# A gate and value stage on five blocks of 768 or 1024 tokens, with its two groups side by side and two of their sums made in PSUM

## The chip, the cores and the metric

One core of a Trainium2 chip runs the whole program. Matrix products run on TensorE (PE in the profile, its weight loads PEld), element-wise work on VectorE (DVE) and ScalarE (ACT), and SyncE (SP) issues the DMA transfers. Operands lie in SBUF, matmuls write to PSUM, which has eight banks of 512 fp32 columns, and large intermediates go through memory. The metric is the device time of one execution in microseconds.

## The reference, cut to what matters

```
x    = attention(q, k, v, g_norm)        # linear attention and RMS norm; 4608 tokens of 512
h    = x @ w_in                          # 512 -> 2048
x    = (h * clip(h + 3, 0, 6) / 6) @ w_out       # 2048 -> 512        (MLP1)
g    = x @ w_gate;  val = x @ w_val      # 512 -> 1536 each          (the stage that is changed)
out  = (silu(g) * val) @ w_out2          # 1536 -> 512                (the output stage)
```

The inputs are float64; the kernel decodes the weights itself.

## The kernel before

Precision comes from splits: a float32 operand is kept as a high and a low part (`h...`, `l...`; L109 on ScalarE makes the high part, L110 on VectorE the low one), and a product is three matmuls, low x high, high x low and high x high. Products of 256 x 256 blocks use a 2 x 2 scheme with seven products for eight: of the x operand seven combinations are needed (B11, B21, B22 and the sums T1 to T4), of the weights seven as well. `product` (L604-613) issues one of the seven: two 128-row pieces of the contraction times three matmuls, six in all.

The program goes through attention, MLP1 in nine blocks of 512 tokens, the gate and value stage, and the output stage in nine blocks of 512. In MLP1's last block the first weights of the next stage are decoded and split (`load_second`), and its last outputs `x1o` are copied from the accumulators `acc_8_0` to `acc_8_3`, the even ones by ScalarE, the odd ones by VectorE (L514-516).

The gate and value stage has six blocks of 768 tokens, in halves of 384 (TH). They are visited forwards with one half of the weights and backwards with the other. At each visit three steps are done, `gv_step`, each for 256 gate and 256 value features: a group `quad` (L721-744) for gate, then one for value. A group is 7 products x 6 matmuls = 42 matmuls of 384 columns in four PSUM banks, so that two groups have all eight. Its sums are made in SBUF: ScalarE copies a product out (L731, L734, L743), VectorE adds the others (L732, L736, L739 to L741). Then come Silu (L748, 1536 columns), the product of both halves (L750, 1536 columns) and the store to `g2d` (L751).

For the next block `load_x1` loads x in one transfer of 1536 KB at the first of a visit's three steps, and `prepare_x` makes sums and splits behind the third. Seven operand pairs lie in the pools `x1` (six tiles, right side of SBUF) and `x2` (eight tiles, left side). Beside the steps, further weights are built (forward half), stored to `wsd` and loaded again at the turn, and the output weights W2 are built (backward half). At the end `g_first` and `g_one` load the output stage's first blocks of `g2d`.

TensorE runs its instructions in the order in which the code issues them; ScalarE's, VectorE's and SyncE's order is set by a scheduler when the program is built. Every engine takes its own in order, so that one that waits holds up all behind it.

## Time and profile before

| | |
|---|---|
| Runs | 1676.84, 1676.83, 1675.19 us; median 1676.83 |
| Profiled execution | 1677.94 us, of which the span of the trace is 1676.1 |
| TensorE busy | 1656.5 us, 99% of the span, 10640 matmuls |
| VectorE, ScalarE busy | 1300.5 us (78%), 851.5 us (51%) |
| Gate and value stage | 864.12 to 1397.60 us after the span's start, 3024 matmuls |

All rows are of the profiled execution. A timeline gives start and duration of each instruction; matmuls overlap in it, since the next starts before the one before has left the array, so that what a matmul costs is the distance between two starts. A name stands without its number (`q_g` for the gate group's banks, `hT` for the high part of a T operand).

### The profile page before, as it was taken

Reading aid. Unit: us, or ns where it says so; the run is one execution under the profiler, and the core shown is the slowest. Engines: PE = TensorE matmul, PEld = TensorE weight load, DVE = VectorE, ACT = ScalarE, POOL = GpSimd, SP = SyncE. Lnnn points to the kernel's source line nnn. Section 1 sums busy time; section 2 is a strip of 40 time slices with the busy share of each in tenths; the row PEclk is TensorE's granted clock in tenths of the full one; section 3 lists DMA queues with packets and bytes.
Section 4 is the critical chain, followed back from the end, with each engine's and each line's share of the span. In section 5 each row is a group of like instructions: output and inputs, shape, how many; then the busy total and the mean of one; then the engine's idle time right before and its main releaser. Section 6 shows DMA issues by size and latency. Waiting matters only on the chain.

```text
span 1676.1 us, 27991 instructions
## 1 busy us (share of the span) xinstructions
PE 1656.5 (99%) x10640; PEld 1526.4 (91%) x10640; DVE 1300.5 (78%) x2472; ACT 851.5 (51%) x1553; POOL 2.4 (0%) x7
## 2 busy tenths in 40 slices
PE   8999999999999999999999999999999999999999
PEld 4567889889989989998889999999999999999999
DVE  6887997677787777777889988678897776877874
ACT  5876554444454444545666555445555444444432
POOL 0000000000000000000000000000000000000000
PEclk9999999999999999999999999999999999999999
DMA  8885444444445454335464544475553357655642
GB/s 231 273 262 163 142 147 136 147 141 147 139 122 160 130 151 119 126 101 201 150 202 163 204 154 157 165 270 194 182 189 131 133 207 275 214 190 195 219 152 101
DMA packets 224998, 288.63 MB, mean 172 GB/s; under 512 B 80992, under 2 KB 139360, under 8 KB 224864
## 3 DMA queue, kind: packets, MB, share of 16 engines
q1 hardware_dynamic: 220480, 285.80, 52.5%
q8 instruction: 83, 1.36, 0.3%
q10 hardware_dynamic: 4384, 1.05, 0.3%
q14 instruction: 51, 0.42, 0.1%
HBM read 211.03 MB, written 75.76 MB: 171 GB/s over the span
## 4 chain that ended last, share of the span: by engine, by line
PE 82%; DVE 9%; DMA 3%; ACT 3%; issue 2%; SPq 0%; DVEq 0%; ACTq 0%
PE q_g L608 14%; PE q_v L608 14%; PE acc L113 7%; PE a L608 7%; PE acc L114 7%; PE acc L115 7%; PE c L608 4%; PE d L608 4%; PE o2c L856 3%; PE o2d L856 3%; PE o2a L856 3%; PE h L119 2%; PE o2e L856 2%; DMA graw<-g2d 1%; PE kv L291 1%
## 5 line engine op out<-in xcount | busy, mean ns | idle before, releaser
L113 PE MATMUL acc<-g,wo 128*128 128x512 f32 x512 | 202.1, 395 | 0.0
L114 PE MATMUL acc<-g,wo 128*128 128x512 f32 x512 | 199.7, 390 | 0.0
L115 PE MATMUL acc<-g,wo 128*128 128x512 f32 x512 | 199.5, 390 | 0.0
L653 ACT ACTIVATE t<-h,three 128x512 f32<-128x512 f32 x120 | 86.9, 724 | 141.4 <-DVE h L650 107.7
L109 ACT ACTIVATE g<-t 128x512 fp32r<-128x512 f32 x142 | 89.5, 630 | 65.3 <-DVE t L654 55.8
L110 DVE TENSOR_TENSOR g<-t,g 128x512 fp32r<-128x512 f32 x142 | 96.7, 681 | 31.6 <-ACT g L109 30.8
L115 PEld LDWEIGHTS acc<-g,wo 128*128 128x128 f32 x512 | 96.1, 188 | 20.4
L113 PEld LDWEIGHTS acc<-g,wo 128*128 128x128 f32 x512 | 96.2, 188 | 20.2 <-DVE g L110 0.4
L114 PEld LDWEIGHTS acc<-g,wo 128*128 128x128 f32 x512 | 96.2, 188 | 18.3
L654 DVE SCALAR_TENSOR_TENSOR t<-t,h 128x512 f32<-128x512 f32 x120 | 82.4, 687 | 30.7 <-ACT t L653 29.3
L608 PE MATMUL q_v<-hT,v 128*128 128x384 f32 x288 | 73.6, 336 | 0.0
L743 ACT ACTIVATE hg<-q_g 128x384 f32<-128x384 f32 x36 | 17.7, 492 | 105.3 <-PE q_g L608 105.3
L750 DVE TENSOR_TENSOR hv<-hg,hv 128x1536 f32<-128x1536 f32 x36 | 63.1, 1753 | 5.5 <-ACT hv L743 5.5
L732 DVE TENSOR_TENSOR h1v<-h1v,q_v 128x384 f32<-128x384 f32 x36 | 19.9, 554 | 54.6 <-ACT h1v L731 53.4
L119 PE MATMUL h<-x,w_i 128*128 128x512 f32 x128 | 57.8, 594 | 1.4 <-DVE w_i L202 0.7
L743 ACT ACTIVATE hv<-q_v 128x384 f32<-128x384 f32 x36 | 17.7, 492 | 79.5 <-PE q_v L608 79.5
L608 PE MATMUL q_v<-hB,v 128*128 128x384 f32 x216 | 55.1, 336 | 0.0
L608 PE MATMUL a<-T,wh_i 128*128 128x256 f32 x240 | 53.4, 285 | 1.6 <-ACT s L627 1.4
L109 ACT ACTIVATE gxh<-gt 128x1024 fp32r<-128x1024 f32 x26 | 27.4, 1054 | 54.0 <-DVE gt L784 54.0
L748 ACT ACTIVATE hg<-hg 128x1536 f32<-128x1536 f32 x36 | 53.5, 1487 | 0.9
L109 ACT ACTIVATE gyh<-gb 128x512 fp32r<-128x512 f32 x54 | 32.3, 623 | 41.2 <-DMA gb<-g2d 40.8
L608 PE MATMUL c<-T,wh_i 128*128 128x256 f32 x240 | 53.0, 283 | 0.0
(618 smaller groups left out, 5460.3 us busy)
## 6 DMA issues: line engine op xcount, KB each, us to landing
wo<-wod SPq DMA_DIRECT2D x128, 512.0 KB, 3.4
g2d<-hv SPq DMA_DIRECT2D x36, 768.0 KB, 3.7
graw<-g2d SPq DMA_DIRECT2D x26, 1024.0 KB, 7.3
xr<-x1d SPq DMA_DIRECT2D x10, 1536.0 KB, 7.1
gb<-g2d SPq DMA_DIRECT2D x54, 256.0 KB, 4.9
x1d<-x1o SPq DMA_DIRECT2D x36, 256.0 KB, 2.8
out_dram<-o SPq DMA_DIRECT2D x36, 256.0 KB, 2.5
raw_i<-in_moe_w_in_dram SPq DMA_DIRECT2D x16, 512.0 KB, 5.5
```

What stands on the lines that cost most here:

```text
L109: nc.scalar.activation(out=hi, in_=src, func=AF.Copy)
L110: nc.vector.tensor_tensor(out=lo, in0=src, in1=f32(hi), op=ALU.subtract)
L113: nc.tensor.matmul(out_, wh, xl, start=start, stop=False)
L114: nc.tensor.matmul(out_, wl, xh, start=False, stop=False)
L115: nc.tensor.matmul(out_, wh, xh, start=False, stop=stop)
L119: nc.tensor.matmul(out_, f32(w), f32(x), start=start, stop=stop)
L608: nc.tensor.matmul(ps, a[:, kk], b[kk] if isinstance(b, list) else b[:, kk], start=first and n == 0, stop=n == 5, skip_group_check=True,)
L653: nc.scalar.activation(out=t, in_=h[i], func=AF.Relu, bias=three[:, 0:1])
L654: nc.vector.scalar_tensor_tensor(out=t, in0=t, scalar=6.0, in1=h[i], op0=ALU.min, op1=ALU.mult)
L748: nc.scalar.activation(out=hg, in_=hg, func=AF.Silu)
L750: nc.vector.tensor_tensor(out=hv, in0=hg, in1=hv, op=ALU.mult)
L856: nc.tensor.matmul(ps[:, i * TO2:(i + 1) * TO2], a[:, cs], b, start=first and i == 0 and n == 0, stop=n == 2, skip_group_check=True,)
```

## The change

The stage now has five blocks, with halves of 384, 512, 512, 384 and 512 tokens (SPANS), ten visits and 30 steps. In a step gate and value are computed together: each of the seven products is issued for gate, then for value, in the order A11 B11, S1 T1, S2 T2, S4 B22, S3 T3, A12 B21, A22 T4, and all eight banks belong to one step. Two sums of a group come about in PSUM: ScalarE copies the bank A to the bank E, on which S2 T2 accumulates, and E to the bank D_, on which S3 T3 and A22 T4 accumulate. VectorE adds two sums a group. Silu and the product of both halves are made for the two odd quarters at once and for the other two one by one, from PSUM. Matmuls on E and D_ never start a bank afresh, so `open_banks` writes these four banks once with `start=True` before the first step. The pool `h` has two buffers for three.

x of the next block comes as eight transfers at the second step of a visit (`load_span`), its sums (`sum_span`) behind that step, and its splits (`split_span`) behind the third. The first block's operands still lie in `x1` and `x2`, which are closed after its third step; two new pools, `xl` (six tiles) and `xr2` (eight), lie over them from then on. Tables (BUILD, RELOAD, W2_AT) say at which steps weights are built, loaded again and made. Three weight halves are stored and loaded again, where it was five: 21 loads, where it was 35. One W2 group is made at a step in full, where it was half a one. Line numbers are shifted by 6 and more: L109, L110 are now L115, L116.

```diff
-    NB2 = NT // T2
+    TW = 512
+    SPANS, t0_ = [], 0
+    for w_ in (TH, TW, TW, TH, TW):
+        SPANS.append((t0_, w_))
+        t0_ += 2 * w_
+    NB2 = len(SPANS)
...
-    def quad(name, w, xo):
-
-        h = big["h"].tile([P, 4, TH], F32, tag="h", name=f"h{name}")
-        u, v = (hpool.tile([P, TH], F32, tag=f"h{i}", name=f"h{i}{name}") for i in range(2))
-
-        a, e, c, d = (
-            big["ps"].tile([P, 512], F32, tag=f"q{i}", name=f"q{i}_{name}")[:, :TH] for i in range(4)
-        )
-        product(c, w["S1"], xo["T1"], True)
-        product(d, w["S3"], xo["T3"], True)
-        nc.scalar.activation(out=v, in_=c, func=AF.Copy)
-        nc.vector.tensor_tensor(out=v, in0=v, in1=d, op=ALU.add)
-        product(a, w["A11"], xo["B11"], True)
-        nc.scalar.activation(out=u, in_=a, func=AF.Copy)
-        product(e, w["S2"], xo["T2"], True)
-        nc.vector.tensor_tensor(out=u, in0=u, in1=e, op=ALU.add)
-        product(c, w["S4"], xo["B22"], False)
-        product(d, w["A22"], xo["T4"], False)
-        nc.vector.tensor_tensor(out=h[:, 3], in0=v, in1=u, op=ALU.add)
-        nc.vector.tensor_tensor(out=h[:, 1], in0=u, in1=c, op=ALU.add)
-        nc.vector.tensor_tensor(out=h[:, 2], in0=u, in1=d, op=ALU.add)
-        product(a, w["A12"], xo["B21"], False)
-        nc.scalar.activation(out=h[:, 0], in_=a, func=AF.Copy)
-        return h
+    def load_span(j):
+
+        t0, w = SPANS[j]
+        x = {}
+        for key, k0, n in (("B12", 0, 1), ("B11", 0, 0), ("B22", 2, 1), ("B21", 2, 0)):
+            for kk in range(2):
+                x[key, kk] = w_slot(f"{key}_{j}_{kk}", F32).rearrange("p k f -> p (k f)")[:, :w]
+                nc.sync.dma_start(
+                    out=x[key, kk], in_=x1d[:, k0 + kk, t0 + n * w:t0 + (n + 1) * w]
+                )
+        return x
+
+    def sum_span(j, x):
+
+        w = SPANS[j][1]
+        for key, a, b in (
+            ("T1", "B12", "B11"), ("T3", "B22", "B12"), ("T2", "B22", "T1"), ("T4", "T2", "B21"),
+        ):
+            for kk in range(2):
+                if key == "T3":
+                    t = x["B12", kk]
+                else:
+                    t = w_slot(f"{key}_{j}_{kk}", F32).rearrange("p k f -> p (k f)")[:, :w]
+                nc.vector.tensor_tensor(out=t, in0=x[a, kk], in1=x[b, kk], op=ALU.subtract)
+                x[key, kk] = t
+
+    def split_span(j, x):
+
+        w = SPANS[j][1]
+        ops = {}
+        for n, key in enumerate(("T1", "T3", "B11", "T2", "B22", "T4", "B21")):
+            pool, m = ("xl", 6) if n < 3 else ("xr", 8)
+            hi, lo = (
+                big[pool].tile([P, 2, TW], F32R, tag="xo", bufs=m, name=f"{o}{key}_{j}")[:, :, :w]
+                for o in "hl"
+            )
+            for kk in range(2):
+                split(hi[:, kk], lo[:, kk], x[key, kk])
+            ops[key] = hi, lo
...
+    def open_banks():
+
+        for n in range(2):
+            for i in (1, 3):
+                o = big["ps"].tile([P, 512], F32, tag=f"q{i}", name=f"open{i}_{n}")
+                w = wgv["g", 0]["A11"][0]
+                nc.tensor.matmul(
+                    o, w[:, 0], wgv_tiles[0].rearrange("p k f -> p (k f)"), start=True, stop=True
+                )
 
     def gv_step(c, j, p, xo):
-        hg = quad(f"g_{c}", wgv["g", p], xo)
-        nc.scalar.activation(out=hg, in_=hg, func=AF.Silu)
-        hv = quad(f"v_{c}", wgv["v", p], xo)
-        nc.vector.tensor_tensor(out=hv, in0=hg, in1=hv, op=ALU.mult)
+
+        t0, th = SPANS[j]
+        hg, hv = (
+            big["h"].tile([P, 4 * TW], F32, tag="h", name=f"h{o}_{c}")[:, :4 * th].rearrange(
+                "p (f c) -> p f c", f=4
+            ) for o in "gv"
+        )
+        v = [hpool.tile([P, TW], F32, tag=f"h{i}", name=f"v{i}_{c}")[:, :th] for i in range(2)]
+        hs, ws = (hg, hv), (wgv["g", p], wgv["v", p])
+        A, E, C, D_ = (
+            [
+                big["ps"].tile([P, 512], F32, tag=f"q{i}", name=f"{o}{i}_{c}")[:, :th]
+                for o in "gv"
+            ] for i in range(4)
+        )
+
+        def prod(ps, a, b, first):
+            for n in range(2):
+                product(ps[n], ws[n][a], xo[b], first)
+                yield n
+
+        for n in prod(A, "A11", "B11", True):
+            nc.scalar.activation(out=E[n], in_=A[n], func=AF.Copy)
+        for n in prod(C, "S1", "T1", True):
+            nc.scalar.activation(out=v[n], in_=C[n], func=AF.Copy)
+        for n in prod(E, "S2", "T2", False):
+            nc.scalar.activation(out=D_[n], in_=E[n], func=AF.Copy)
+            nc.scalar.activation(out=hs[n][:, 1], in_=E[n], func=AF.Copy)
+        for n in prod(C, "S4", "B22", False):
+            nc.vector.tensor_tensor(out=hs[n][:, 1], in0=hs[n][:, 1], in1=C[n], op=ALU.add)
+        for n in prod(D_, "S3", "T3", False):
+            nc.vector.tensor_tensor(out=hs[n][:, 3], in0=D_[n], in1=v[n], op=ALU.add)
+        odd = slice(1, 4, 2)
+        nc.scalar.activation(out=hg[:, odd], in_=hg[:, odd], func=AF.Silu)
+        nc.vector.tensor_tensor(out=hv[:, odd], in0=hg[:, odd], in1=hv[:, odd], op=ALU.mult)
+        for ps, a, b, o in ((A, "A12", "B21", 0), (D_, "A22", "T4", 2)):
+            for n in prod(ps, a, b, False):
+                if n == 0:
+                    nc.scalar.activation(out=hg[:, o], in_=ps[0], func=AF.Silu)
+                else:
+                    nc.vector.tensor_tensor(out=hv[:, o], in0=hg[:, o], in1=ps[1], op=ALU.mult)
         nc.sync.dma_start(
-            out=g2d[2 * p:2 * p + 2, :, j * T2:(j + 1) * T2].rearrange("f p t -> p f t"),
+            out=g2d[2 * p:2 * p + 2, :, t0:t0 + 2 * th].rearrange("f p t -> p f t"),
             in_=hv.rearrange("p (f n) c -> p f (n c)", f=2),
...
         mlp1.close()
-        big["x2"] = mlp2.enter_context(tc.tile_pool(name="x2", bufs=1, reuse_waits="tile"))
-        big["h"] = mlp2.enter_context(tc.tile_pool(name="h", bufs=3, reuse_waits="tile"))
+        big["h"] = mlp2.enter_context(tc.tile_pool(name="h", bufs=2, reuse_waits="tile"))
+        big["x2"] = gv1.enter_context(tc.tile_pool(name="x2", bufs=1, reuse_waits="tile"))
         big["ps"] = ctx.enter_context(tc.tile_pool(name="ps", bufs=2, space=PSUM, reuse_waits="tile"))
         x_ops[0] = next(parts)
+        open_banks()
...
+        BUILD = {1: (1, 0), 3: (1, 1), 4: (2, 0), 6: (2, 1), 7: (3, 0), 9: (3, 1), 10: (4, 0),
...
+        W2_AT = {16: 0, 18: 1, 19: 2, 21: 3, 22: 4, 24: 5}
...
+            if i == 1 and nxt != j:
+                x1 = load_span(nxt)
             gv_step(c, j, p, x_ops[j])
             while second:
                 load_second()
+            if i == 1 and nxt != j:
+                sum_span(nxt, x1)
             if i == NH - 1 and nxt != j:
-                *_, x_ops[nxt] = prepare_x(nxt, x1)
-            if n < NB2:
-                m = (n + 1) % NB2
-                if i < 2:
-                    tiles = load_half(*halves[m], i)
-                    if i and m:
-                        for k, t in enumerate(tiles):
-                            nc.sync.dma_start(
-                                out=wsd[m - 1, k], in_=f32(t).rearrange("p k f -> p (k f)")
-                            )
-                    elif i:
-                        wgv[halves[0]] = operands(tiles)
-                if n == turn:
-                    for m in (2 * i + 1, 2 * i + 2):
-                        if m < 2 * NH:
-                            reload(m)
-            else:
-
-                m = c - NB2 * NH
-                if m < W2_STEPS:
-                    tiles = make_w2(m // 2, m % 2)
-                    if tiles:
-                        for k, t in enumerate(tiles):
-                            nc.sync.dma_start(out=w2d[m // 2, k], in_=flat(f32(t)))
+                if n == 0:
+                    gv1.close()
+                    big["xl"] = mlp2.enter_context(
+                        tc.tile_pool(name="xl", bufs=1, reuse_waits="tile")
+                    )
+                    big["xr"] = mlp2.enter_context(
+                        tc.tile_pool(name="xr2", bufs=1, side="right", reuse_waits="tile")
+                    )
+                x_ops[nxt] = split_span(nxt, x1)
```

The change moves instructions on ScalarE and TensorE where the stage begins. On ScalarE, before: `x1o` are the copies of the last accumulators, `w_v4` to `y_v5` decode two value weights, `hT`, `hB` are splits of x.

```order
L516 ACTIVATE x1o_10042<-acc_8_0_9187 128x512
L516 ACTIVATE x1o_10048<-acc_8_2_9195 128x512
L187 ACTIVATE w_v4_10212<-raw_v4_10210 128x512
L109 ACTIVATE hT4_0_10081<-T4_0_0_10067 128x384
L109 ACTIVATE hT4_0_10081<-T4_0_1_10069 128x384
L166 ACTIVATE y_v4_10214<-raw_v4_10210,half_95 128x512
L109 ACTIVATE hB21_0_10087<-xr_0_9103 128x768
L187 ACTIVATE w_v5_10220<-raw_v5_10218 128x512
```

The same place on ScalarE now:

```order
L522 ACTIVATE x1o_10042<-acc_8_0_9187 128x512
L193 ACTIVATE w_v4_10216<-raw_v4_10214 128x512
L172 ACTIVATE y_v4_10218<-raw_v4_10214,half_95 128x512
L193 ACTIVATE w_v5_10224<-raw_v5_10222 128x512
L115 ACTIVATE hT2_0_10071<-T2_0_0_9878 128x384
L115 ACTIVATE hT2_0_10071<-T2_0_1_9880 128x384
L172 ACTIVATE y_v5_10226<-raw_v5_10222,half_95 128x512
L522 ACTIVATE x1o_10048<-acc_8_2_9195 128x512
```

The second copy, of `acc_8_2`, was next to the first; now six instructions stand between, four of the decoding and two splits.

On TensorE, the last matmuls of MLP1 and the first of the stage, before:

```order
L113 MATMUL acc_8_3_9199<-g_8_15_9958,wo_15_9963 128x512
L114 MATMUL acc_8_3_9199<-g_8_15_9958,wo_15_9963 128x512
L115 MATMUL acc_8_3_9199<-g_8_15_9958,wo_15_9963 128x512
L608 MATMUL q2_g_0_10098<-lT1_0_9863,wh_g0_1_9237 128x384
L608 MATMUL q2_g_0_10098<-hT1_0_9862,wl_g0_1_9238 128x384
L608 MATMUL q2_g_0_10098<-hT1_0_9862,wh_g0_1_9237 128x384
```

And now, where `open...` are the four matmuls of `open_banks`, `g0_0` is bank A of gate in step 0:

```order
L119 MATMUL acc_8_3_9199<-g_8_15_9958,wo_15_9963 128x512
L120 MATMUL acc_8_3_9199<-g_8_15_9958,wo_15_9963 128x512
L121 MATMUL acc_8_3_9199<-g_8_15_9958,wo_15_9963 128x512
L765 MATMUL open1_0_10091<-wh_g0_0_9233 128x512
L765 MATMUL open3_0_10093<-wh_g0_0_9233 128x512
L765 MATMUL open1_1_10095<-wh_g0_0_9233 128x512
L765 MATMUL open3_1_10097<-wh_g0_0_9233 128x512
L614 MATMUL g0_0_10103<-lB11_0_9875,wh_g0_0_9233 128x384
L614 MATMUL g0_0_10103<-hB11_0_9874,wl_g0_0_9234 128x384
```

The four write the PSUM banks in which `acc_8_0` to `acc_8_3` lay, and stand ahead of the first product.

On ScalarE at the first change of blocks, now: `hg_2` is made by the Silus of the first block's last step, `g1_3` is a copy of the next block's first step.

```order
L808 ACTIVATE hg_2_10404<-g3_2_10414 128x384
L115 ACTIVATE hT4_1_10559<-T4_1_0_10392 128x512
L115 ACTIVATE hT1_1_10529<-T1_1_0_10382 128x512
L115 ACTIVATE hT1_1_10529<-T1_1_1_10384 128x512
L115 ACTIVATE hT3_1_10535<-B12_1_0_10251 128x512
L115 ACTIVATE hT3_1_10535<-B12_1_1_10253 128x512
L115 ACTIVATE hB11_1_10541<-B11_1_0_10255 128x512
L115 ACTIVATE hB11_1_10541<-B11_1_1_10257 128x512
L115 ACTIVATE hT4_1_10559<-T4_1_1_10394 128x512
L115 ACTIVATE hB21_1_10565<-B21_1_0_10263 128x512
L115 ACTIVATE hB21_1_10565<-B21_1_1_10265 128x512
L792 ACTIVATE g1_3_10577<-g0_3_10575 128x512
```

Before, in the same place, `h0v_2` and `hv_2` are copies of the first block's last step and `h1g_3` the first of the next block's:

```order
L731 ACTIVATE h1v_2_10468<-q2_v_2_10471 128x384
L109 ACTIVATE hT1_1_10541<-T1_1_0_10525 128x384
L109 ACTIVATE hT1_1_10541<-T1_1_1_10529 128x384
L734 ACTIVATE h0v_2_10467<-q0_v_2_10469 128x384
L109 ACTIVATE hT3_1_10547<-T3_1_0_10527 128x384
L109 ACTIVATE hT3_1_10547<-T3_1_1_10531 128x384
L109 ACTIVATE hT2_1_10557<-T2_1_0_10533 128x384
L109 ACTIVATE hB11_1_10553<-xr_1_10091 128x768
L109 ACTIVATE hT2_1_10557<-T2_1_1_10537 128x384
L166 ACTIVATE y_g8_10700<-raw_g8_10696,half_95 128x512
L187 ACTIVATE w_g9_10823<-raw_g9_10821 128x512
L743 ACTIVATE hv_2_10466<-q0_v_2_10469 128x384
```

T1, T3 and B11 were split between the copies of the last step; now they are split behind its last Silu.

## Rows read from the trace of the kernel before

**Rows 1.** The page, busy time of each engine: us (share of the span) and instructions.
```profile
PE 1656.5 (99%) x10640; PEld 1526.4 (91%) x10640; DVE 1300.5 (78%) x2472; ACT 851.5 (51%) x1553; POOL 2.4 (0%) x7
```

**Rows 2.** Busy us by stretch, the whole stage: PE, PEld, DVE, ACT, POOL, PEclk, DMA.
```profile
864.12:1397.60 533.48, 532.73 (x3026) 527.76 (x3024) 430.51 (x762) 268.14 (x474) 0.00 (x0) 1.00 0.52 184
```

**Rows 3.** Timeline of TensorE where the stage begins: start us, us, instruction.
```profile
862.76 0.39 PE L113 MATMUL acc<-g,wo 128*128 128x512 f32 x1
...
864.12 0.34 PE L608 MATMUL q_g<-lT,wh_g 128*128 128x384 f32 x1
...
867.12 0.34 PE L608 MATMUL q_g<-hB,wh_g 128*128 128x384 f32 x1
...
868.17 0.34 PE L608 MATMUL q_g<-hT,wh_g 128*128 128x384 f32 x1
868.56 0.44 PE L608 MATMUL q_g<-lB,wh_g 128*128 128x384 f32 x1
868.84 0.34 PE L608 MATMUL q_g<-hB,wl_g 128*128 128x384 f32 x1
```

**Rows 4.** The same view inside a later step.
```profile
1105.26 0.34 PE L608 MATMUL q_g<-lT,wh_g 128*128 128x384 f32 x1
...
1107.17 0.33 PE L608 MATMUL q_g<-hB,wh_g 128*128 128x384 f32 x1
```

**Rows 5.** Timeline of ScalarE there; in brackets idle time before and releaser.
```profile
863.64 0.60 ACT L516 ACTIVATE x1o<-acc 128x512 f32<-128x512 f32 x1 [0.77 <-PE acc L115]
864.67 0.68 ACT L187 ACTIVATE w_v<-raw_v 128x512 f32<-128x512 f32 x1 [0.43 <-DMA raw_v<-in_moe_w_val_dram]
865.25 0.92 ACT L109 ACTIVATE hT<-T 128x384 fp32r<-128x384 f32 x2
866.08 0.75 ACT L166 ACTIVATE y_v<-raw_v,half 128x512 uint32<-128x512 uint16 x1
866.73 0.83 ACT L109 ACTIVATE hB<-xr 128x768 fp32r<-128x768 f32 x1
...
868.02 0.49 ACT L731 ACTIVATE h1g<-q_g 128x384 f32<-128x384 f32 x1
```

**Rows 6.** Timeline of VectorE there.
```profile
865.21 0.68 DVE L514 TENSOR_SCALAR x1o<-acc 128x512 f32<-128x512 f32 x1
865.81 1.02 DVE L110 TENSOR_TENSOR lT<-T,hT 128x384 fp32r<-128x384 f32 x2
...
869.01 0.68 DVE L173 SCALAR_TENSOR_TENSOR w_v<-raw_v,w_v 128x512 uint32<-128x512 uint32 x1
869.61 0.69 DVE L170 SCALAR_TENSOR_TENSOR w_v<-w_v,y_v 128x512 uint32<-128x512 uint32 x1
```

**Rows 7.** Timeline of VectorE at a step's end.
```profile
985.98 1.75 DVE L750 TENSOR_TENSOR hv<-hg,hv 128x1536 f32<-128x1536 f32 x1
987.65 0.55 DVE L732 TENSOR_TENSOR h1g<-h1g,q_g 128x384 f32<-128x384 f32 x1
```

**Rows 8.** The page, DMA issues: count, KB each, median us from issue to landing.
```profile
g2d<-hv SPq DMA_DIRECT2D x36, 768.0 KB, 3.7
```

**Rows 9.** Timeline of ScalarE, two splits of 512 columns in a row.
```profile
1400.11 1.15 ACT L109 ACTIVATE gyh<-t 128x512 fp32r<-128x512 f32 x2
```

**Rows 10.** Timeline of VectorE, two splits of 512 columns in a row.
```profile
1415.19 1.29 DVE L110 TENSOR_TENSOR gyl<-gb,gyh 128x512 fp32r<-128x512 f32 x2
```

**Rows 11.** Waits of TensorE, stage and output entry: us in total, times, longest.
```profile
PE o2c L856 <- DVE gyl L110: 0.8, 1, 0.8
```

**Rows 12.** Timeline of ScalarE where the output stage waits for data.
```profile
1413.93 1.31 ACT L109 ACTIVATE gyh<-gb 128x512 fp32r<-128x512 f32 x2 [2.59 <-DMA gb<-g2d]
```

**Rows 13.** Busy time by stretch at the output stage's entry.
```profile
1404.00:1416.00 12.00, 11.21 (x94) 11.01 (x93) 6.90 (x10) 4.26 (x6) 0.00 (x0) 1.00 1.04 388
```

**Rows 14.** Timeline of TensorE at the run's start and one pass later.
```profile
5.02 0.91 PE L291 MATMUL kv<-vA,kA 128*64 128x64 f32 x12 [5.02 <-DMA vA<-in_v_dram]
...
12.76 0.91 PE L291 MATMUL kv<-vA,kA 128*64 128x64 f32 x12
```

More of the change, by code (lines that the diff above doesn't have):

```diff
@@ L666, with prepare_x @@
     x_ops = {}
[L668 to L682 removed]
+    def x_op(name):
+        return big["x" if len(x_ops_made) < 6 else "x2"].tile(
+            [P, 2, TH], F32R, tag="xo", bufs=6 if len(x_ops_made) < 6 else 8, name=name
+        )
+    x_ops_made = []
+    def prepare_x(j, x):
         b11, b12 = x[:, 0:2, :TH], x[:, 0:2, TH:]
@@ new lines, in split_span @@
+    def split_span(j, x):
[10 more added lines that the diff above has]
+            ops[key] = hi, lo
+        return ops
@@ L1224 @@
                         ph1.__exit__(None, None, None)
+                        gv1 = ExitStack()
                         big["xr"], raw2, big["x"] = (
-                            mlp2.enter_context(tc.tile_pool(name=o, bufs=1, side="right"))
+                            gv1.enter_context(tc.tile_pool(name=o, bufs=1, side="right"))
                             for o in ("xr", "raw2", "x1")
@@ L1271, in reload_w2, with build @@
             w2_operands(q, tiles)
+        BUILD = {1: (1, 0), 3: (1, 1), 4: (2, 0), 6: (2, 1), 7: (3, 0), 9: (3, 1), 10: (4, 0),
+                 13: (0, 1), 14: (5, 0), 15: (5, 1)}
+        RELOAD = {12: (1,), 13: (2, 3), 14: ()}
+        W2_AT = {16: 0, 18: 1, 19: 2, 21: 3, 22: 4, 24: 5}
+        def build(m, i, keep):
+            tiles = load_half(*halves[m], i)
+            if tiles and keep:
+                wgv[halves[m]] = operands(tiles)
+            elif tiles:
+                for k, t in enumerate(tiles):
+                    nc.sync.dma_start(
+                        out=wsd[m - 1, k], in_=f32(t).rearrange("p k f -> p (k f)")
+                    )
         for c, (n, j, p) in enumerate(steps):
```

45 lines of the change are left out of this document (23 added, 22 removed).

## The prediction

> **What bounds the kernel now.** I read the page first, then busy time by stretch, then TensorE's timeline at the joints of the stage that is changed, and last ScalarE's and VectorE's timelines there. TensorE is busy for 1656.5 of 1676.1 us [rows 1], and the gate and value stage is a stretch of 533.48 us at full granted clock [rows 2] in which VectorE (430.5 us) and ScalarE (268.1 us) have room. So time in this stage has only two prices: what the matmuls cost, by number and columns, and the places where TensorE stands still.
>
> The matmul price comes from start-to-start distances. The six 512-column matmuls from 862.76 to 864.12 start 1.36/6 = 0.2267 us apart [rows 3]. The 384-column ones from 1105.26 to 1107.17 start 1.91/11 = 0.1736 us apart [rows 4]; the stage's fast stretches average 0.1733, which I use. The difference over 128 columns is 0.417 ns a column, and 160.0 ns of 173.3 or 213.3 of 226.7 are columns: about 13.3 ns come with each matmul whatever its width. Some matmuls are a little slower: from 864.12 to 867.12, 17 distances of 0.1765 [rows 3]. These are the first three products of a group, whose x operands lie in another pool than the rest, 18 of each group's 42, so 1296 in all at 3.2 ns: 4.1 us. Of the 533.48 us the 3024 matmuls are 3024 x 0.1733 = 524.1 and the slow ones 4.1; the remaining 5.3 us are gaps. One is seen at 868.17, 868.56, 868.84, where 0.39 and 0.28 stand for 0.17 each [rows 3]. The usual cause in later steps is the product of both halves, 1.75 us on VectorE, ahead of the sum that frees a PSUM bank [rows 7].
>
> **The change, part by part, against the profiled run (1677.94 us; the median of the runs is 1676.83, 1.1 less).**
>
> *Number of matmuls.* Before: 36 steps x 2 groups x 42. After: 30 x 84 = 2520, of which 1008 have 384 columns and 1512 have 512. The columns are the same, 1,161,216, and 504 matmuls x 13.3 ns go: **-6.7 us**. The Trainium skill, "TensorE: Matmul & The Clock Gate", section "Wait — 56ns, not 53.3ns?", gives a fixed cost of about 2.5 ns per matmul at full clock; by that the term would be -1.3 us, an estimate from that page. The rows leave 13 ns at either width, five times as much, and I keep them.
>
> *Slow reads.* In the new pools 1404 matmuls, 864 of them 512 wide, read operands on the side where I saw 3.2 ns more. At 3.2 ns each that is 4.5 against 4.1 (+0.4), and if it grows with the width 5.4 (+1.3). I take **+0.8**. If the pool is not the cause it could be -4.1 or twice that; both ends stay for the range.
>
> *Steps inside a block.* Five VectorE sums a group become two; ScalarE gets two copies from PSUM to PSUM a group, on which matmuls then accumulate. With g and v side by side a copy has three products to be done: 3 x 6 x 0.173 = 3.1 us at 384 columns, 4.1 at 512, against a copy of 0.49 [rows 5] (0.60 for 512) and some 0.2 us behind the product's end. Slack 2.4 or 3.3 us, where today the 1.75 us product stands in front of a bank's release. A copy into PSUM has no row; between 0 and twice the copy into SBUF it stays within the slack, so its price is 0. Banks and hv are now single: the store of hv is issued just behind the step's last product and lands 3.7 us later [rows 8], about 4.7 us into the next step, while the first write to the new hv comes after its sixth product, 6.2 us (8.2). What covers it is 1.5 us; a landing later than that delays a copy that itself has slack. So of the 5.3 us of gaps I leave 0.5 as jitter and 1.0 for the seven later block switches, where splits and last weights sit in the same queues: **-3.8** (bounds: all gaps gone, -5.3; 1.5 us at each of seven switches, +5.2).
>
> *Entry.* Four new matmuls open the banks that are never started afresh, right behind MLP1's last one, and they write the banks of the last accumulators acc_8_0 to acc_8_3. ScalarE frees acc_8_0 and acc_8_2. Before, both copies stood together (the second at 863.64 [rows 5]), nothing on TensorE waited for them, and products started at 864.12 in other banks. Now decode steps of two weights and two splits stand between: the second copy comes after w_v, y_v, w_v, two hT, y_v. The first w_v cannot start before its data, 864.67 [rows 5]. From starts in that list: w_v 0.58, y_v 0.65, two hT 0.83. So 864.67 + 0.58 + 0.65 + 0.58 + 0.83 + 0.65 = 867.96, plus 0.60 for the copy: 868.56. VectorE frees acc_8_3 behind two decode steps of 0.60 and two lT of 0.47 [rows 6]; the first can start when y_v ends, 866.0, so 866.0 + 1.2, then 2 x 0.47 = 868.15, plus 0.68: 868.85. The last opening matmul then runs 0.23, and the first product starts near 869.1 where it was 864.12: **+5.0**. The early gap of this place is in the 5.3 already taken off. Lower bound 2.5 (copies early by the data's landing), upper 6.
>
> *First switch.* The first block's operands lie in two pools that are closed after its third step, and the new pools lie over them. Before, B11 was the third product of a step and its splits sat among the previous step's work; now B11 is first and its split stands behind T4, T1 and T3 on ScalarE, and behind T1 and T3 on VectorE. A step of 384 columns is 84 x 0.1733 = 14.56 us. ScalarE's last Silu of g needs product 13, 13.52 + 0.2, and leaves at 14.1; five splits of 512 at 0.53 (two in 1.15 [rows 9]) bring it to 16.75. VectorE follows one behind: T1 at 15.3 and 15.9, T3 at 16.5 and 17.1 (0.60 each, two in 1.29 [rows 10]), B11's first half at 17.7 to 18.4. The next step could have started at 14.56. **+4.0** (bounds 3 and 5).
>
> *Output stage's entry.* Its first blocks of g now load later, since their slots are in the x operands' pool and the transfers queue behind the last stores. Before, TensorE waited 0.8 us there for gyl [rows 11], ScalarE 2.59 us for gb [rows 12], and the DMA moved 388 GB/s at a share of 1.04 from 1404 to 1416 [rows 13], so moved transfers are not hidden there. Going through the queue in its new order I find 0.5, 0.3 and 1.8 us of waits against 1.3: **+1.5** (bounds 0 and +4, the latter if the 1024 KB load comes two places later).
>
> Weight builds and reloads move (21 reloads for 35), in stretches where the DMA share is 0.52 [rows 2]: 0, or in the price of the switches.
>
> Sum: -6.7 + 0.8 - 3.8 + 5.0 + 4.0 + 1.5 = +0.8 us. The profiled run would read 1678.7, the median **1677.6**.
>
> **Rivals.**
> - *The slow reads go.* If the 3.2 ns come from what else touched that memory in those products and not from the pool, 4.1 us leave instead of 0.8 coming: 1677.6 - 4.9 = 1672.7. For it: the slow pitch is in the first products of a group alone. Against: it goes with one pool in every step I looked at.
> - *The queues are late at every switch (slower side).* Fourteen splits of 512 on ScalarE (7.4 us) and on VectorE (8.4 us) go in among the step's own copies in the order of the program. Where they put a copy more than 2.4 us (3.3 at 512) late, TensorE stands, since all eight banks are in use. At 1.5 us more on each of seven switches it is +10.5 - 1.0: 1687. For it: VectorE is 81% busy over the stage. Against: its sums shrink from ten to four a step.
> - *The output entry costs its upper bound*, 4 instead of 1.5: 1680.1.
> - *The clock falls in the two new idle stretches of about 4 us.* Where the run begins, twelve kv matmuls behind 5.02 us of idleness took 0.91 us, and the same twelve a pass later, behind busy work, 0.91 too [rows 14]: no lower clock is seen. If matmuls ran at 1.2 instead of 2.4 GHz for as long as each idle stretch, each would lose 2 us: 1681.6. The Trainium skill, "TensorE: Matmul & The Clock Gate", section "Part 1: The HAM clock gate", says that an idle TensorE falls to half clock and gets it back only after busy time; by that rule this is what would happen, and rows 14 speak against it.
> - *The edit doesn't save what it says*: if what a matmul costs beside its columns were a fifth of 13.3 ns, and the columns dearer for it (0.2302 us for 512), the first term would be -1.3: 1683.0. The six matmuls of MLP1 at 0.2267 [rows 3] speak against it.
>
> **How the numbers follow.** Chances: forecast 0.42, reads 0.16, late queues 0.22, output entry 0.10, clock 0.06, no saving 0.04. The likeliest case has its own range, 1674.5 to 1681, from the bounds of entry, first switch and output stage (about 3 us either way taken together). To hold 8 in 10 I reach to most of the reads case and to nearly all of the late queues: 1671.8 to 1686. Within 0.2% is 1673.5 to 1680.2, about what a measurement of this kernel can tell from no change. Faster: the reads case with the forecast's low tail, 0.20. Same: most of the forecast and half of the output case, 0.45. Slower: 0.35.
>
> **What would show it.** Each step right: 2520 matmuls between the first product and the output stage, distances of 0.227 at 512 columns; TensorE idle from about 865 to 869 behind the x1o copies; one idle stretch of about 4 us some 44 us later before B11's first matmul, released by VectorE; no wait above 0.3 us inside other steps; 2 to 3 us of waits for gb or graw at the output's entry. Wrong: a third idle stretch of over 1 us in the stage, waits for the PSUM copies in ordinary steps, or a granted clock below 1.00.

## The result, and the profile after

The changed kernel takes 1684.97 us (median of four runs, 1683.76 to 1687.48) against 1676.82: a ratio of 1.0053, 95% interval 1.0041 to 1.0065. It is slower by 8 us, where the forecast was 1677.6 and no measurable change. The time lies within the stated range, near the rival of late queues (1687), but the queues were not late. The profiled run took 1683.76 us.

TensorE's line of the page, which answers [rows 1]:

```profile
PE 1654.3 (98%) x10140; PEld 1462.1 (87%) x10140; DVE 1204.2 (72%) x2272; ACT 884.9 (53%) x1633; POOL 2.5 (0%) x7
```

The matmuls are 500 fewer in the whole program (504 fewer in the products, four more that open banks), and TensorE's busy time falls by 2.2 us instead of 6.7. The stage as one stretch, then three short stretches in it (columns as in [rows 2]):

```profile
861.99:1401.80 539.81, 532.32 (x2525) 464.16 (x2524) 332.69 (x560) 302.17 (x559) 0.00 (x0) 0.99 0.46 163
864.00:868.00 4.00, 2.07 (x6) 1.83 (x7) 3.61 (x8) 3.43 (x7) 0.00 (x0) 0.78 0.95 314
868.00:870.00 2.00, 2.00 (x8) 2.00 (x8) 2.00 (x4) 0.64 (x2) 0.00 (x0) 0.58 1.00 342
917.00:920.00 3.00, 3.00 (x10) 2.34 (x9) 3.00 (x6) 1.10 (x3) 0.00 (x0) 0.58 0.00 0
```

The stage is 6.3 us longer than before, and the granted clock is 0.58 on average over two short stretches, where it was 1.00 throughout. TensorE's waits in the stage and the output stage's entry, which answer [rows 11]:

```profile
PE g L614 <- DVE lB L116: 3.9, 1, 3.9
PE open L765 <- ACT x1o L522: 3.6, 1, 3.6
PE o2c L916 <- DMA 25_3_14859<-w2d: 2.2, 1, 2.2
PE o2c L916 <- DVE gxl L116: 0.5, 1, 0.5
```

These are the three places that the prediction named, at nearly its prices, and no fourth: no block switch but the first appears. At the output's entry, though, the longest wait is for `25_3`, a part of W2, and not for a block of g. TensorE's timeline at the entry, which answers [rows 3]:

```profile
861.99 0.39 PE L765 MATMUL open<-wh_g 128*128 128x512 f32 x1
865.93 1.39 PE L765 MATMUL open<-wh_g 128*128 128x512 f32 x3 [3.55 <-ACT x1o L522]
867.12 0.52 PE L614 MATMUL g<-lB,wh_g 128*128 128x384 f32 x1
867.44 0.52 PE L614 MATMUL g<-hB,wl_g 128*128 128x384 f32 x1
...
869.36 0.48 PE L614 MATMUL v<-hB,wl_v 128*128 128x384 f32 x1
869.68 0.34 PE L614 MATMUL v<-hB,wh_v 128*128 128x384 f32 x1
869.85 0.34 PE L614 MATMUL v<-lB,wh_v 128*128 128x384 f32 x1
```

The first opening matmul runs at once, the other three 3.9 us later, and the first product starts 5.13 us after the opening began. Then eight matmuls start 0.32 us apart, which is 384 columns at the lower level of the clock (1.2 GHz), before the distance becomes 0.17. ScalarE's timeline there, which answers [rows 5], shows what the opening waited for:

```profile
861.37 0.66 ACT L193 ACTIVATE w_v<-raw_v 128x512 f32<-128x512 f32 x1 [0.63 <-DMA raw_v<-in_moe_w_val_dram]
...
865.28 0.60 ACT L522 ACTIVATE x1o<-acc 128x512 f32<-128x512 f32 x1 [0.57 <-DMA x1d<-x1o]
```

The copy of the last even accumulator starts 3.9 us behind the first decode step, with the four decode steps and two splits between them. TensorE's timeline at the first change of blocks:

```profile
912.10 0.51 PE L614 MATMUL v<-hT,n_v 128*128 128x384 f32 x2
916.54 0.50 PE L614 MATMUL g<-lB,wh_g 128*128 128x512 f32 x1 [3.94 <-DVE lB L116]
...
918.09 0.63 PE L614 MATMUL g<-hB,wh_g 128*128 128x512 f32 x1
918.51 0.63 PE L614 MATMUL v<-lB,wh_v 128*128 128x512 f32 x1
...
921.22 0.40 PE L614 MATMUL g<-hT,wl_g 128*128 128x512 f32 x1
921.45 0.40 PE L614 MATMUL g<-hT,wh_g 128*128 128x512 f32 x1
```

Again an idle stretch of 4 us, and behind it distances of 0.427, which is 512 columns at 1.2 GHz; then 0.23. In the middle of the stage two products of one step read differently. First S1 T1, then S4 B22, start of gate's and of value's first matmul:

```profile
1101.57 0.39 PE L614 MATMUL g<-lT,wh_g 128*128 128x512 f32 x1
...
1102.93 0.39 PE L614 MATMUL v<-lT,wh_v 128*128 128x512 f32 x1
...
1107.11 0.39 PE L614 MATMUL g<-lB,wh_g 128*128 128x512 f32 x1
...
1108.51 0.39 PE L614 MATMUL v<-lB,wh_v 128*128 128x512 f32 x1
```

Six matmuls take 1.36 us with T1 (0.2267 each) and 1.40 with B22 (0.2333). Sorted by product over all 512-column steps, without the stretches of waiting and half clock, the mean distance is 226.9 ns for S1 T1, S4 B22 and A22 T4 233.3, S2 T2 and A12 B21 234.6, and some 230 for A11 B11 and S3 T3, each behind slow ones: they start slow and recover.

### The profile page after: what moved, and what is told of

It reads as the page before. It is cut to its first block, busy times and chain, and to the rows that moved or that the text cites. A ratio compares the mean times of both kernels' runs of the same rounds, so it can differ in the third digit from the quotient of the medians.

```text
span 1681.9 us, 26849 instructions
## 1 busy us (share of the span) xinstructions
PE 1654.3 (98%) x10140; PEld 1462.1 (87%) x10140; DVE 1204.2 (72%) x2272; ACT 884.9 (53%) x1633; POOL 2.5 (0%) x7
## 4 chain that ended last, share of the span: by engine, by line
PE 90%; DVE 5%; DMA 3%; ACT 1%; issue 1%; SPq 0%; DVEq 0%; ACTq 0%
PE g L614 16%; PE v L614 16%; PE acc L119 7%; PE acc L120 7%; PE acc L121 7%; PE a L614 7%; PE o2a L916 4%; PE o2d L916 4%; PE o2c L916 4%; PE c L614 4%; PE d L614 4%; PE h L125 2%; PE o2e L916 2%; PE kv L297 1%; DMA raw_v<-in_moe_w_val_dram 1%
## 5 line engine op out<-in xcount | busy, mean ns | idle before, releaser
L115 ACT ACTIVATE g<-t 128x512 fp32r<-128x512 f32 x142 | 89.5, 630 | 65.9 <-DVE t L660 56.5
L116 DVE TENSOR_TENSOR g<-t,g 128x512 fp32r<-128x512 f32 x142 | 96.7, 681 | 31.6 <-ACT g L115 30.8
L799 DVE TENSOR_TENSOR hg<-hg,g 128x512 f32<-128x512 f32 (+1 forms) x30 | 19.0, 633 | 96.1 <-PE g L614 91.9
L803 ACT ACTIVATE hg<-hg 128x1024 f32<-128x1024 f32 (+1 forms) x30 | 29.2, 974 | 70.1 <-DVE hg L801 70.0
L810 DVE TENSOR_TENSOR hv<-hg,v 128x512 f32<-128x512 f32 (+1 forms) x60 | 38.0, 633 | 36.5 <-PE v L614 35.0
L808 ACT ACTIVATE hg<-g 128x512 f32<-128x512 f32 (+1 forms) x60 | 33.2, 553 | 58.1 <-PE g L614 57.8
L614 PE MATMUL g<-lB,wh_g 128*128 128x512 f32 (+1 forms) x150 | 56.5, 376 | 3.9 <-DVE lB L116 3.9
L614 PE MATMUL g<-hB,wl_g 128*128 128x512 f32 (+1 forms) x150 | 56.5, 377 | 0.0
L614 PE MATMUL g<-hB,wh_g 128*128 128x512 f32 (+1 forms) x150 | 56.4, 376 | 0.0
L115 ACT ACTIVATE gxh<-gt 128x1024 fp32r<-128x1024 f32 x26 | 27.5, 1057 | 54.2 <-DVE gt L844 53.6
L614 PE MATMUL g<-hT,wl_g 128*128 128x512 f32 (+1 forms) x150 | 55.8, 372 | 0.0
L614 PE MATMUL g<-lT,wh_g 128*128 128x512 f32 (+1 forms) x150 | 55.6, 371 | 0.0
L614 PE MATMUL g<-hT,wh_g 128*128 128x512 f32 (+1 forms) x150 | 55.5, 370 | 0.0
```

What stands on the lines that cost most here:

```text
L115: nc.scalar.activation(out=hi, in_=src, func=AF.Copy)
L116: nc.vector.tensor_tensor(out=lo, in0=src, in1=f32(hi), op=ALU.subtract)
L614: nc.tensor.matmul(ps, a[:, kk], b[kk] if isinstance(b, list) else b[:, kk], start=first and n == 0, stop=n == 5, skip_group_check=True,)
L808: nc.scalar.activation(out=hg[:, o], in_=ps[0], func=AF.Silu)
L810: nc.vector.tensor_tensor(out=hv[:, o], in0=hg[:, o], in1=ps[1], op=ALU.mult)
```

## The experiments

All kernels below are the changed kernel with the edit shown, unless the text says otherwise. The stage's duration is taken from the first matmul behind MLP1 to the first of the output stage; it was 533.5 us before and 539.8 after. The theory to begin with: the 8 us are two idle stretches, the clock that falls in them, and slower reads of x; the rival was that something in the new pattern itself is slow.

**1. Keep TensorE busy in the idle stretches.**

```diff
+                for _ in range(15 if (n, i) == (0, 1) else 0):
+                    nc.tensor.matmul(
+                        o, w[:, 0], wgv_tiles[0].rearrange("p k f -> p (k f)"),
+                        start=True, stop=True
+                    )
...
+        for _ in range(17 if c == NH else 0):
+            nc.tensor.matmul(
+                A[0], ws[0]["A11"][0][:, 0], kept[0].rearrange("p k f -> p (k f)"),
+                start=True, stop=True
+            )
```

> The changed kernel with matmuls that compute nothing needed in its two long idle stretches: 15 more of the first bank-opening matmul at the stage's entry, and 17 into gate's first bank at the first change of blocks, about 3.6 and 3.9 us of matmuls where TensorE stood still for 3.7 and 4.1 us. Theory (the idle stretches make the granted clock fall, and 11 to 14 matmuls behind each then run at half clock): the waits end where they ended, the granted clock stays 1.00, matmuls behind the waits start 0.175 and 0.23 us apart at once, and 3.8 us go: 1680.0 against 1683.8. Rival (the clock falls for another reason, as the new pattern of matmuls begins): the half-clock stretches stay and the time is 1683.8 or more.

Measured: 1683.65 us (ratio to before 1.0042, 1.0027 to 1.0057), stage 537.8. TensorE's timeline at the entry:

```profile
864.38 3.56 PE L771 MATMUL open<-wh_g 128*128 128x512 f32 x15
868.46 0.96 PE L767 MATMUL open<-wh_g 128*128 128x512 f32 x3 [0.51 <-ACT x1o L522]
869.26 0.34 PE L614 MATMUL g<-lB,wh_g 128*128 128x384 f32 x1
869.43 0.34 PE L614 MATMUL g<-hB,wl_g 128*128 128x384 f32 x1
```

The first product comes 5.1 us behind the opening's start, as late as without the extra matmuls, but the distances are 0.17 at once, and the granted clock of the whole run is 1.00 (0.998 before). So idleness is what lowers the clock. The stage gains 2.0 us and not the 3.8 expected: in the first step the copies to PSUM, hidden while the matmuls ran slowly, now come 1.0 us late (four short waits between 873.3 and 875.4). The theory holds for the mechanism, and half for the price; the median, 1.3 us less, does not tell more.

**2. Open the banks behind three products.**

```diff
-        open_banks()
...
+        for n in prod(C, "S1", "T1", True):
+            if n == 0 and not c:
+                for i in range(2):
+                    open_bank(banks[1][i])
+                    nc.scalar.activation(out=E[i], in_=A[i], func=AF.Copy)
+                for i in range(2):
+                    open_bank(banks[3][i])
```

> The changed kernel with the four bank-opening matmuls moved behind the first three products of the first step (A11 B11 of gate and value, S1 T1 of gate), which need banks that are free. Theory: these 3.1 us of work run while ScalarE and VectorE free the last accumulators, so the wait of 3.6 us shrinks to under 1 us, the clock does not fall there, and 4.8 us go (5.13 of opening and waiting become 1.5, and 1.2 of half clock go): 1679.0 against 1683.8; the wait at the first change of blocks and its half clock stay. Rival (what is gained at the entry is given back where copies into the opened banks come late): 1682 or more, with a new wait of 2 us or more at S2 T2 in the first step.

Measured: 1682.66 us (ratio 1.0039, 1.0024 to 1.0053), stage 537.0; 2.8 us less of it where 4.8 were expected. TensorE's waits at the entry:

```profile
PE g L761 <- ACT x1o L522: 1.3, 1, 1.3
...
PE g L614 <- ACT g L794: 0.8, 1, 0.8
```

3.6 us became 1.3, and 0.8 came back at S2 T2 for gate's copy, which waits for the opened bank. The median is where the rival had it (1682 or more), but its wait at S2 T2 is 0.8 us and not 2 or more. No half clock follows at the entry; the first change of blocks is as it was.

**3. The same, and the splits in the order of their use.** The tiles of a pool are taken first, then B11 is split before T1.

```diff
-        for n, key in enumerate(("T1", "T3", "B11", "T2", "B22", "T4", "B21")):
...
+        for key in ("B11", "T1", "T2", "B22", "T3", "B21", "T4"):
```

> As the run before (banks opened behind three products), and at each change of blocks the x operands are split in the order of their use, B11 first, instead of third. Theory: at the first change B11's first half is split on ScalarE right behind one other split and on VectorE right behind the last product of both halves, so the wait of 4.1 us becomes about 1.4, the clock stays at 1.00 in the whole stage, and 2.7 + 1.9 us more go: 1674.4, below the kernel before (1676.8). What is left against a stage of ideal matmuls is then the slow reads of about 10 us. Rival (T1 or T3 now come late instead of B11): the wait moves to S1 T1 or S3 T3 of the same step with 2 us or more, 1677 or more.

Measured: 1678.69 us (ratio 1.0014, 1.0004 to 1.0023), stage 532.3, where the kernel before has 533.5. The wait for lB is 1.5 us, as expected, and the stage's clock is full. But the time missed its number by 4 us. Of these, 2.0 were missing in run 2 already; the timeline of TensorE in the output stage shows a further part:

```profile
1411.25 0.38 PE L922 MATMUL o2c<-25_3_14855,gxh 128*128 128x256 f32 x1 [2.27 <-DMA 25_3_14855<-w2d]
...
1412.34 0.41 PE L922 MATMUL o2d<-24_4_14842,gxl 128*128 128x256 f32 x1
1412.55 0.41 PE L922 MATMUL o2d<-24_4_14842,gxh 128*128 128x256 f32 x1
```

Behind 2.3 us of waiting, matmuls of 256 columns start 0.213 us apart, the lower level of the clock once more, and 1.4 us go there. In the profiles of the changed kernel and of run 2 the same wait left the clock alone. So part of the scatter of these kernels' runs is whether the clock falls behind a wait: of the ten runs, the three with a granted clock of 1.00 took 1677.6 to 1677.8 us, the one with 0.997 took 1681.2.

**4. The x pools on the other sides of SBUF.**

```diff
-                        tc.tile_pool(name="xl", bufs=1, reuse_waits="tile")
+                        tc.tile_pool(name="xl", bufs=1, side="right", reuse_waits="tile")
...
-                        tc.tile_pool(name="xr2", bufs=1, side="right", reuse_waits="tile")
+                        tc.tile_pool(name="xr2", bufs=1, reuse_waits="tile")
```

> The changed kernel with the two pools of x operands of all blocks but the first on the other sides of SBUF: T1, T3, B11 (six tiles) at the high addresses on the right, T2, B22, T4, B21 (eight tiles) at the low ones on the left. Now 512-column matmuls of S1 T1 start 226.9 ns apart, of S2 T2, S4 B22, A12 B21, A22 T4 233 to 235. Theory (the address of the x operand decides): S1 T1 and later matmuls of A11 B11 and S3 T3 rise to 233 to 235, and those of S4 B22, A12 B21, A22 T4 fall to 227 apart from the first ones after a change of pool; in all about 2 us less. Rival (the product decides, as those that add to a bank's contents are slower): the distances by product stay as they are, and so does the time.

Measured: 1677.73 us in one run. S1 T1 and S4 B22, gate's and value's first matmul, as above:

```profile
1099.25 0.39 PE L614 MATMUL g<-lT,wh_g 128*128 128x512 f32 x1
...
1100.65 0.39 PE L614 MATMUL v<-lT,wh_v 128*128 128x512 f32 x1
...
1104.81 0.39 PE L614 MATMUL g<-lB,wh_g 128*128 128x512 f32 x1
...
1106.17 0.39 PE L614 MATMUL v<-lB,wh_v 128*128 128x512 f32 x1
```

Now T1 has 1.40 and B22 1.36. The products have changed places, so it is the place of the x operand and not the product. Beside it the wait at the first change of blocks fell to 1.5 us, and 25_3 was not waited for; why was not followed up, so the time says nothing about the reads. But one tile of the left pool now reached up to 182,624 and was as fast as the others there, where a tile from 179,136 on had been slow: the addresses, which the compiled program gives, did not divide into low and high. What divided them was the address modulo 64: all tiles on the left, the weights too, are at 32, all on the right at 0.

**5 to 8. Shift one side by a few bytes.** Both kernels already hold a tile of 32 bytes at the base of the right side, `pad32`, that nothing reads. These runs add a second one there (5, and 7 in the kernel before), or one on the left side (6, one more constant, which moves the tiles behind it by 32 bytes), or the right one with the edits of run 3 (8).

```diff
+    pad = ctx.enter_context(tc.tile_pool(name="pad", bufs=1, side="right"))
+    pad.tile([P, 8], F32, tag="pad", name="pad")
     hpool = ctx.enter_context(tc.tile_pool(name="h1", bufs=1, side="right"))
...
+    const.tile([P, 1], F32, name="pad")
```

> The changed kernel with one more tile of 32 bytes a partition at the base of the right side of SBUF, so that all tiles on that side start 32 bytes lower: their addresses become 32 modulo 64, as the left side's are (weights, xl), where they were 0. So far x operands on the right gave 512-column distances of 231 to 240 ns (mean 233 to 235), those on the left 226.7. Theory A (the x operand is slow where its address and the weights' differ modulo 64): S2 T2, S4 B22, A12 B21 and A22 T4 fall to 226.7 to 227, about 9.8 us go from the stage, 1674 against 1683.8 (the two idle stretches and the half clock stay). Theory B (the right side, or addresses above about 179,000, are slow): nothing changes, 1683.8.

> The changed kernel with one more tile of 32 bytes at the base of the left side: weights and xl become 0 modulo 64, as the right side is. Theory A (a difference between weights and x operand modulo 64 is what costs): all distances at 512 columns fall to 226.7, as with the pad on the right, 1674. Theory A2 (an x operand at 0 modulo 64 is slow, whatever the weights' address): all seven products are slow, 233 or more, the stage some 6 us longer, 1690. Theory B (the side): nothing changes.

> The kernel before with one more tile of 32 bytes at the base of the right side. Its operands T1, T3 and B11 lie there. Theories A and A2: the matmuls of S1 T1, S3 T3 and A11 B11, now 174 to 180 ns apart (mean 176.5), fall to 173.3, and 4.1 us go: 1672.5 against 1676.5. Theory B: no change.

> The changed kernel with the banks opened behind three products, the splits in the order of use (both runs as tried together before, 1678.7) and the pad on the right. Theory A or A2: 9.8 us less than that, 1669, some 7 us below the kernel before; the waits of the output stage's entry (2.4 and 0.7 us) stay. Theory B: 1678.7.

Measured: right 1682.70 us (ratio 1.0039, 1.0024 to 1.0053), left 1679.82 (one run), the kernel before with the pad 1673.42 (ratio 0.9986, 0.9977 to 0.9995), run 3 with the pad 1672.74 (0.9980, 0.9970 to 0.9989). S4 B22 with the pad on the right:

```profile
1109.40 0.39 PE L616 MATMUL g<-lB,wh_g 128*128 128x512 f32 x1
...
1110.78 0.39 PE L616 MATMUL v<-lB,wh_v 128*128 128x512 f32 x1
```

Six take 1.38: neither 1.40 nor 1.36. The mean of the 512-column distances falls from 231.8 to 229.5 ns, that of 384 columns from 175.7 to 173.8, and the pad on the left does the same to each product within 0.6 ns (on the mean over gate or value). So theory B falls (the side did not change) and A2 falls (x at 0 modulo 64 is fast when the weights are there too): what costs is a difference of phase between x and weights. No run moved the weights without the left x tiles; that the weights are the partner rests on S4 B22, whose six matmuls read x on the right alone and are slow at each position. But where four fifths of the slowness went at 384 columns, less than half of it went at 512, and a step of the theory is missing. Run 5's median gains only 2.3 us, where 9.8 were expected: its profile has half clock behind three waits, at the entry, the first change of blocks and the output stage, and once more at 61.8 us, behind a wait of 1.9 us, with a granted clock of 0.994 in all. Run 6 shows more of the gain, with a stage of 534.2 us. In the kernel before, the right side's products fall to 172.5 to 173.3 ns and the stage from 533.5 to 531.0, less than the 4.1 us expected, since S2 T2, the first on the other side, rises from 174.0 to 176.1. Runs 7 and 8 are below the kernel before.

**9 and 10. The phase modulo 128, and the W2 loads ahead.** Right tiles stood at 32 modulo 128 with the pad, weights and left tiles at 96. Run 9 is run 8 with a pad of 96 bytes, which brings the right tiles to 96 too; run 10 also issues one group of loads earlier.

```diff
-    pad.tile([P, 8], F32, tag="pad", name="pad")
+    pad.tile([P, 24], F32, tag="pad", name="pad")
...
+        reload_w2(4)
         mlp2.close()
...
         prepare_g(1)
-        reload_w2(4)
```

> As the run with late opening, splits in order of use and a pad on the right side (1672.7), but with a pad of 96 bytes instead of 32. With 32 bytes the 512-column distances on x operands at the right side fell from a mean of 233.3 to 228.8 ns, not to 226.7. There the right side's tiles are at 32 modulo 128, the left side's and the weights at 96. Theory A3 (the same phase modulo 128 is what counts): with 96 bytes all are at 96 modulo 128 and all distances at 512 columns fall to 226.7, about 3 us less, 1669.7. Rival (the remaining 2 ns belong to the side or to other tiles): the distances stay at 228.8 and the time at 1672.7.

> As best96, and the seven loads of the fifth W2 group for the output stage are issued ahead of the second block of g, in the queue ahead of it and of the last store. Theory: the wait of 2.3 us for 25_3 in the output stage becomes under 0.5, since its loads then go some 5 us earlier; 2 us less than best96. Rival (the transfers are bound by the DMA's rate there, 388 GB/s before): the wait moves to gb or graw of the next unit, and the time stays.

Measured: 1668.63 us (ratio 0.9957, 0.9941 to 0.9974) and 1665.46 us (0.9937, 0.9922 to 0.9952). S4 B22 in run 9, last matmul of T2's product and then gate's six of B22, three of them shown:

```profile
1097.58 0.39 PE L616 MATMUL v<-hT,wh_v 128*128 128x512 f32 x1
1097.81 0.39 PE L616 MATMUL g<-lB,wh_g 128*128 128x512 f32 x1
1098.03 0.39 PE L616 MATMUL g<-hB,wl_g 128*128 128x512 f32 x1
1098.26 0.39 PE L616 MATMUL g<-hB,wh_g 128*128 128x512 f32 x1
```

The distances are 0.22 to 0.23, and by their means 226.6 to 226.8 ns in all of S2 T2, S4 B22, S3 T3, A12 B21 and A22 T4, at each position: the slow reads are gone. A pad lowers the right side's tiles by its size, and in the changed kernel as it is they stand at 64 modulo 128; so without `pad32` they would stand at 96 as well. By these addresses it is this tile, in both kernels, that sets the sides apart; no run leaves it out. Run 10, busy time of the stage:

```profile
863.59:1386.10 522.51, 519.68 (x2525) 459.21 (x2524) 331.20 (x560) 301.23 (x559) 0.00 (x0) 1.00 0.49 172
```

And TensorE's waits in run 10, in the stage and at the output's entry:

```profile
PE g L616 <- DVE lB L118: 1.6, 1, 1.6
PE g L765 <- ACT x1o L524: 0.7, 1, 0.7
PE o2c L924 <- DVE gxl L118: 0.6, 1, 0.6
PE g L616 <- ACT g L798: 0.6, 1, 0.6
```

The stage is 17.3 us shorter than in the changed kernel, the wait for 25_3 is gone, the output stage is 2.6 us shorter than in run 9, and the clock is full. This is the fastest version, 10.5 us below the kernel before. Not all of it belongs to the new form: the kernel before has 4.6 us of slow reads itself, and no run gives it the pad of 96 bytes.

**11 and 12. Six blocks of 384 in the new form,** first in the changed kernel, then in run 10.

```diff
-    for w_ in (TH, TW, TW, TH, TW):
+    for w_ in (TH,) * 6:
...
```

The tables of weight steps (BUILD, RELOAD, W2_AT) move along.

> The changed kernel with six blocks of 768 tokens, all halves 384, in 36 steps of the new form (weight steps moved along); 3024 matmuls as in the kernel before. Theory: against the changed kernel 1512 matmuls of 512 columns at a mean of 231.8 become 2016 of 384 at 175.7, +3.7 us, the wait at the first change of blocks is 1 us shorter (splits of 384), so its stage is 2 to 4 us longer than 539.8 us, less what the clock does. So the wider blocks are worth 3.7 us here and not 6.7, since half the gain went into slower reads. Rival (all of the 504 x 13.3 ns is kept): 6 us longer. Rival (wider blocks save nothing): 538.5 to 539.

> As best96o (1665.5), with six blocks of 768 tokens in place of the five. All operands have the weights' phase now, so the slow reads are out of the comparison, and both should have their clock. Theory (13.3 ns come with each matmul): 504 more matmuls cost 6.7 us, less about 0.7 for a shorter first change of blocks: 1671.5. Rival (what a matmul costs beside its columns is a fifth of that): 1666.

Measured: 1692.47 us in one run, stage 544.7; and 1671.34 us (ratio to before 0.9972, 0.9961 to 0.9982), stage 528.6. The first is 4.9 us longer in its stage than the changed kernel, a little above the 2 to 4 expected, with 10 and 17 matmuls at half clock behind its two waits where the changed kernel has 8 and 7, so that it tells little. The second is 6.1 us longer in its stage than run 10, at full clock in both: 504 matmuls cost about what the first term said (6.7 us, here less a first change of blocks that is 0.3 us shorter).

## Where the prediction held and where it failed, by its own steps

The forecast was no change, with +0.8 us; the two profiled runs differ by 5.8, the medians by 8.2 (two of the four runs of the changed kernel, 1686.17 and 1687.48 us, have granted clocks of 0.997 and 0.996 where the profiled one has 0.998). Between the profiled runs the changed kernel reached the stage 2.1 us earlier, at 861.99. In the other kernels' profiles the same place lies between 861.9 and 865.5, with the same work ahead of it, so this is scatter and no effect of the change. From there on it loses 7.9 us: 6.3 in the stage, 1.1 in the output stage's matmuls, and 0.5 behind the last.

| Term | Predicted | Found | How |
|---|---|---|---|
| Number of matmuls | -6.7 | -6.6 | 2520 at 173.3 and 226.7 ns against 3024 at 173.3 |
| Slow reads | +0.8 | +5.4 | 10.1 us above those distances, 4.6 before, to 0.1 |
| Steps inside a block | -3.8 | -4.6 | 0.2 us of gaps left of 4.8 |
| Entry | +5.0 | +4.7 | 5.13 without 0.4 of half clock |
| First switch | +4.0 | +4.2 | idle of 4.1 and the restart |
| Clock | 0 | +3.2 | 2 openings, 8 and 7 matmuls at 1.2 GHz, two in between |
| Output stage | +1.5 | +1.6 | 1.1, and 0.5 at the end |

**Two terms failed.** *Slow reads*: the prediction tied them to a pool, took 3.2 ns a matmul from 384 columns, and let it grow with the width to 1.3 us at most. The matmuls on the side that it named were slow, but by 6.6 ns at 512 columns, and those behind them were slow too. The cause was not the pool as such but the tiles' phase modulo 128 against the weights' (runs 4 to 9). The range allowed for "twice that"; the value came from the narrower 0.4 to 1.3. *Clock*: it was put at nothing because [rows 14] were read as evidence that 5 us of idleness do not lower it. That reading fails. The trace of the kernel before goes on:

```profile
14.03 2.08 PE L119 MATMUL ss<-sq,ones 128*128 128x512 f32 x2
...
16.91 0.57 PE L291 MATMUL kv<-vA,kA 128*64 128x64 f32 x12
...
18.14 1.02 PE L119 MATMUL ss<-sq,ones 128*128 128x512 f32 x2
```

The twelve kv matmuls of the next pass take 0.57 us and not 0.91, and two `ss` matmuls 1.02 where they took 2.08. So both groups in [rows 14] ran at the lower level of the clock, though the view gives 1.00 for that time, and comparing them could not show that idleness is harmless. In the middle of dense work a wait of 3.6 us was followed by half clock, and so were all the others of 3.1 to 4.0 us in the profiles of this stage. The rival had 0.06 and a price of 4.0 us; it happened and cost 3.2. The Trainium skill, "TensorE: Matmul & The Clock Gate", section "Part 1: The HAM clock gate", has the rule that an idle TensorE falls to half clock and gets it back after busy time. By that rule the stretches behind both waits were to be expected, and run 1 agrees, since it kept TensorE busy and the clock at 1.00.

**Luck.** That the time lies in the range owes something to luck: the upper end was stretched for the late queues, and what filled it were the two terms above.

**Right were** the count (run 12: 6.1 us for 504 matmuls less a shorter switch), the two idle stretches with their releasers (3.6 and 3.9 us), the smooth steps, and the price of the output's entry: 2.2 and 0.5 us of waits where 0.5, 0.3 and 1.8 were summed. The path there was another: the prediction had TensorE wait for blocks of g, and it waited longest for a load of W2. Run 10 issued that group earlier, and the wait went. The rival of late queues did not occur: seven switches cost 0.2 us together. Not settled is why half clock follows the output's wait of some 2 us in some profiles and not in others.

## What to carry to other kernels

Where many matmuls run a few nanoseconds longer than their columns ask, compare the addresses of moving and stationary operands modulo 128 before looking for contention; here, with the rest unchanged, a pad of 96 bytes beside `pad32` was worth 4 us over one of 32 bytes, and 10 over `pad32` alone. A small tile that nobody reads can itself be what sets the phases apart. Where TensorE stood still for 3.1 to 4.0 us in dense matmul work, that was paid twice, once as the wait and once as half clock behind it, so put independent matmuls in front of the waiting one. Before two groups of matmuls are taken as proof of full clock, compare them with the same matmuls at a place where the distances show it. When work is regrouped, look at the order in which each engine frees the first step's banks and fills the first step's operands: inside the blocks the waits went as planned, and the loss was at joints, in the clock behind them and in addresses.

## What the runs showed of the hardware that was not expected

With x and weights in the same phase modulo 128, 512-column matmuls start 226.7 ns apart; with x at 64 and weights at 96 the means of S4 B22 are 231 to 237, by position in the product, and with 32 against 96 (run 5), or 64 against 0 (run 6), they are 226 to 232. At 384 columns the smaller loss is nearly nothing (a mean of 173.8 ns over the stage), the larger 2.4 ns. The slowness outlasts the operand: in the changed kernel A11 B11 and S3 T3, on good addresses behind bad ones, still have 231 ns for gate's six matmuls and 228 for value's.

At 1.2 GHz the distances are 320 and 427 ns, exactly the columns; the 13.3 ns of a matmul at full clock do not show there.

A copy of 512 columns by ScalarE from one PSUM bank to another, for which the prediction had no row, takes 0.58 us in the changed kernel, against 0.59 from PSUM into SBUF.
